# A head-major layout for score blocks that pass through DRAM, half as many small transfers, and a new written-out order in a recurrence kernel

## The chip, the core and the metric

One core of a Trainium2 chip runs the whole program. Its engines are TensorE (PE; PEld is its weight load), VectorE (DVE), ScalarE (ACT), GpSimd (POOL) and SyncE (SP). Each has its own instruction queue and works through it in order; they wait for each other through semaphores. DMAs are issued from the queues of SP, ACT and POOL and all run on the core's 16 DMA engines. The metric is the device time of one execution in microseconds (us), as the median of several runs.

## The reference

Three stages follow each other: a recurrence over 768 time steps, an attention with four experts, and a gated MLP with a mixing over time. The change touches the first.

```python
def _attn_ref(r, k, v, w, a, b):          # all [4, 8, 768, 40]
    state = zeros((B, H, D, D))
    for t in range(S):
        y[:, :, t] = einsum('bhd,bhde->bhe', rt, state)
        Sa = einsum('bhde,bhe->bhd', state, at)
        state_decay = state * wt[:, :, None, :] - einsum('bhd,bhe->bhde', Sa, bt)
        state = state_decay + einsum('bhd,bhe->bhde', vt, kt)
# x = y as [4, 768, 320]
# moe:  per expert e of 4: causal softmax attention (head width 64), ye = a @ v @ wo[e], top-2 gated sum
# moe2: h = relu(x @ w_in); u, v = halves; v_n = layer norm of v; (u * (w_spatial @ v_n + b)) @ w_out
```

## The kernel before, in words

The recurrence is computed in 12 steps g of 64 time positions. Each step has two half-steps s = 2g and 2g + 1 (two of the four batch entries each, side by side on the partitions), so there are 24 half-steps.

**Preparation of a half-step s.** POOL issues the loads `xw`, `xa`, `xk`. DVE computes the running products of the decays (`scan`, L171), `at` (L176), a reciprocal (L179), the scan backwards (`back`, L181) and `kb` (L186). PE computes the 64x64 score blocks of eight heads (`t`, L195: 64 matrix products that run two by two, so the order prints 32 of a pair as x32) and transposes `kb` (`x`, L235). ACT copies the blocks out of PSUM (`lb`, L207, into `la` and `lb`) and stores both to a DRAM tensor (`lo`, L212); SP fetches them from there (`l`, L223) into the tile `ls`, in which each partition holds one 32x32 matrix. DVE masks the other half of the blocks (`lk`, L200).

**Inversion.** Two steps form a unit k (SIZES), six in all. When the four half-steps of a unit have been fetched, POOL masks the matrices (`lm`, L227), and DVE inverts 128 triangular matrices at once in 30 rows, two instructions each (`sub`, L252 and L254). ACT transposes half of them (`xc`, L259) and stores them (`xo`, L267).

**The step g.** SP fetches the inverses into the tiles G and R (`gx`, L273). PE and ACT combine them (`ma` L281, `mae`, `mb` L294, `mbe` L299). The state goes from step to step through `lv` (L306), `w` (L312), `we` (ACT, L317), `u` (L324), `ue` (ACT, L330), `s` (L341) and `state` (DVE, L348 and L349). The outputs need `st` (L355), `vt` (L369), `vte` (ACT), `a` (L386, two pieces of 64 products), `am` (DVE, L391, two), `ys` (L402), `yk` (L411), `xs` (DVE, L418) and the store `out` (SP, L1072) to the DRAM tensor `xd`.

**What sets the order.** `Plan` (L34) is given every piece with an engine, a guessed cost and a due time, and writes out one order for each engine: among the pieces that could begin within SLACK of the earliest, the one that is due first. REACH is the guessed time until a transfer's data can be used, PEC a factor on the costs of PE's pieces, DUE the numbers from which the due times are made. The order is fixed when the program is built; on the chip, an engine whose next instruction has to wait waits.

Besides, each DMA that SP or ACT issues takes one of eight completion counters in turn (DMAHW0 to DMAHW7 in the rows of the order), and waits until the DMA that had this counter eight DMAs earlier has landed. These waits stand in the queue of the issuing engine.

After the recurrence, the weights of the attention (L589 to L642 on DVE, prepared while its last steps run) and then attention and MLP follow; they read `xd` one batch entry after the other (L735, L766).

Of the kernel before, what the change touches and what calls it, by code (L numbers as in the profile page):

```python
# [7 lines left out]
F32 = mybir.dt.float32  # L8
# [13 lines left out]
CT = 64  # L22
SIZES = (2,  2,  2,  2,  2,  2)
RINGS = {"f": 4, "xw": 3, "xa": 2, "xk": 2, "kb": 1, "rp": 1, "pp": 12, "at": 9, "lk": 9, "la": 3, "lb": 10, "kbt": 11, "ls": 2, "lt": 1, "xt": 1, "wsb": 1,
       "s0": 1, "rt": 1, "vut": 2, "am": 2, "xs": 1}
DUE = {"pace": 21.6, "lead": 66.3, "half": 2.6, "out": 1.0, "sub": 17.1, "row": 1.50, "turn": 17.7, "gx": 23.3, "load": 6.0, "init": 10.0}
LAG_US = 0.2
REACH = {"xw": 5.2, "xa": 5.2, "xk": 5.2, "v": 6.2, "r": 6.2, "lo": 5.5, "l": 5.5, "xo": 5.2, "gx": 5.7, "init": 1.2}
SLACK = 0.1
PEC = 0.71  # L30
QPR = 8


class Plan:  # L34
# [5 lines left out]
    def add(self, name, engine, cost, due, fn, needs=(), makes=None, uses=()):  # L40

        self.items[name] = [engine, cost * PEC if engine == "PE" else cost, due, fn, list(needs) + list(uses), makes, list(uses)]

    def order(self):
# [9 lines left out]
        def begin(n):  # L54
            engine, _, _, _, needs, makes, _ = items[n]
            if makes and len(rings[makes]) >= self.cap[makes]:
                needs = needs + readers.get(rings[makes][-self.cap[makes]], [])
                if any(u not in at for u in needs):
                    return None
            return max([free.get(engine, 0.0)] + [at[u] + REACH.get(u[0], 0.0 if items[u][0] == engine else LAG_US)  # L60
                                                  for u in needs])

        open_ = [n for n in items if not missing[n]]
        while open_:
            can = [(t, items[n][2], i, n) for i, n in enumerate(open_) for t in (begin(n),) if t is not None]
            first = min(can)[0]

            _, _, t, n = min((due, i, t, n) for t, due, i, n in can if t <= first + SLACK)
            free[items[n][0]] = at[n] = t + items[n][1]
# [11 lines left out]
def recurrence(ctx, tc, shape, x_in, rt_in, v_in, ident, store_x, pre=None):  # L81


    nc = tc.nc
    B, H, S, D = shape
    C, L2 = CT, CT // 2
# [9 lines left out]
    dp = ctx.enter_context(tc.tile_pool(name="rdram", bufs=1, space=DRAM))  # L96
# [3 lines left out]
    starts = [sum(SIZES[:k]) for k in range(len(SIZES))]  # L100
    unit_of = [k for k, n in enumerate(SIZES) for _ in range(n)]

    XW, XA, XK, LA, LO, PP, AT, KBT, KB, LK, LB, XT, RT, VU = ({} for _ in range(14))
    LS, LT, XO, pw, wsb, aq, rp = ({} for _ in range(7))
# [102 lines left out]
            nc.scalar.copy(d[s], aq["t", s][:, 1].rearrange("p (h t) -> p h t", h=H)[:, :, i * L2:(i + 1) * L2])  # L207

    def p_lo(s):
        LO[s] = dp.tile([2, 2, C, H, L2], F32, name=f"lo{s}")  # L210
        for i, t in enumerate((LA[s], LB[s])):
            nc.scalar.dma_start(LO[s][i].rearrange("y j h t -> (y j) h t"), t)  # L212

    def p_l(s):

        k = unit_of[s // 2]
        n = SIZES[k] * 32
        if k not in LS:
            LS[k] = ap.tile([128, L2, L2], F32, name="ls", bufs=RINGS["ls"])
        for y in range(2):  # L220
            for i in range(2):
                at0 = i * n + (s // 2 - starts[k]) * 32 + y * 16 + s % 2 * H
                nc.sync.dma_start(LS[k][at0:at0 + H], LO[s][i, y, i * L2:(i + 1) * L2].rearrange("j h t -> h j t"))  # L223

    def p_lm(k):
        n = 2 * SIZES[k] * 32
# [34 lines left out]
    def p_xo(g):  # L261
        k = unit_of[g]
        n = SIZES[k] * 32
        at0 = (g - starts[k]) * 32
        XO[g] = dp.tile([2, 2, 2 * H, L2, L2], F32, name=f"xo{g}")
        for i, t in ((1, LS[k][n:2 * n]), (0, LT[k][:n])):
            nc.scalar.dma_start(XO[g][i].rearrange("y n l t -> (y n) (l t)"), t[at0:at0 + 32].rearrange("n l t -> n (l t)"))  # L267

    def load_x(g):

        for y in range(2):
            for i, t in enumerate((G, R)):
                nc.sync.dma_start(t[rows(2 * y + i), :, i * L2:(i + 1) * L2],  # L273
                                  XO[g][i, y].rearrange("n l t -> l n t"))

    def m_a(g):
        aq["ma", g] = pt = bank2()
# [145 lines left out]
    add = plan.add  # L423
    last = NS - 1
    add(("init", 0), "POOL", 14.5, DUE["init"], lambda: init())
    for k, n in enumerate(SIZES):
        due = DUE["pace"] * starts[k] - DUE["lead"]
        ss = range(2 * starts[k], 2 * (starts[k] + n))
        for s in ss:
            d = due - DUE["half"] * (ss[-1] - s)  # L430
            add(("xw", s), "POOL", 1.2, d - DUE["load"], lambda s=s: load_w(s), makes="xw")
            add(("xa", s), "POOL", 1.2, d - DUE["load"] + 1, lambda s=s: load_a(s), makes="xa")
            add(("xk", s), "POOL", 2.4, d - DUE["load"] + 2, lambda s=s: load_k(s), makes="xk")
            add(("scan", s), "DVE", 1.27, d, lambda s=s: scan(s), makes="pp", uses=[("xw", s)])
            add(("at", s), "DVE", 0.65, d, lambda s=s: at(s), makes="at", uses=[("xa", s), ("scan", s)])
            add(("back", s), "DVE", 1.45, d, lambda s=s: back(s), [("scan", s)], makes="rp", uses=[("xw", s)])
            add(("kb", s), "DVE", 1.24, d, lambda s=s: kb(s), makes="kb", uses=[("xk", s), ("back", s)])
            free = [(n, (s - RINGS[r]) // 2) for n, r in (("ma", "lb"), ("lv", "lk"), ("w", "at")) if s >= RINGS[r]]
            add(("t", s), "PE", 1.75, d, lambda s=s: p_t(s), free, makes="f", uses=[("kb", s), ("at", s)])
            free = [("lo", s - RINGS["la"])] if s >= RINGS["la"] else []  # L440
            add(("lb", s), "ACT", 0.75, d, lambda s=s: p_lb(s), free, makes="lb", uses=[("t", s)])
            add(("lk", s), "DVE", 0.7, d, lambda s=s: p_lk(s), [("lb", s)], makes="lk", uses=[("t", s)])
            free = [("xo", starts[k - RINGS["ls"] + 1] - 1)] if k >= RINGS["ls"] else []
            add(("lo", s), "ACT", 0.8, d, lambda s=s: p_lo(s), uses=[("lb", s)])
            add(("l", s), "SP", 2.2, d, lambda s=s: p_l(s), free + [("lo", s)])
            free = [("yk", (s - RINGS["kbt"]) // 2, q2) for q2 in range(2) if s >= RINGS["kbt"]]
            add(("x", s), "PE", 1.45, d + 2, lambda s=s: p_x(s), free, makes="f", uses=[("kb", s)])
            add(("xe", s), "ACT", 0.8, d + 2, lambda s=s: p_xe(s), makes="kbt", uses=[("x", s)])
        add(("lm", k), "POOL", 1.8, due + DUE["sub"], lambda k=k: p_lm(k), [("l", s) for s in ss])
        for j in range(1, L2 - 1):  # L450
            add(("sub", k, j), "DVE", 0.32 + 0.0022 * (L2 - 1 - j) * j, due + DUE["sub"] + DUE["row"] * j, lambda k=k, j=j: sub(k, j),
                [("sub", k, j - 1) if j > 1 else ("lm", k)])
        free = [("xo", starts[k] - 1)] if k else []
        add(("xc", k), "ACT", 2.0, due + 30, lambda k=k: p_xc(k), [("sub", k, L2 - 2)] + free)
        for g in range(starts[k], starts[k] + n):
            add(("xo", g), "ACT", 0.8, due + 30, lambda g=g: p_xo(g), [("xc", k)])
    for g in range(NS):
        due, k, e, o = DUE["pace"] * g, unit_of[g], (2 * g, 2 * g + 1), DUE["pace"] * (g + 1) + DUE["out"]
# [10 lines left out]
            uses=[("lk", s) for s in e])  # L469
# [10 lines left out]
        for q2 in range(2):  # L480
# [5 lines left out]
                uses=[("am", g, q2), ("xe", 2 * g + q2)])  # L486
        add(("ys", g), "PE", 1.5, o + 2, lambda g=g: ys(g), [("a", g, 1), ("am", g, 0)], makes="f",
            uses=[("r", g), ("ste", g)])
        add(("xs", g), "DVE", 1.3, o + 3, lambda g=g: xs(g), [("yk", g, 0), ("yk", g, 1)], makes="xs",
            uses=[("ys", g)] + [("scan", s) for s in e])  # L490
        add(("out", g), "SP", 2.4, o + 3, lambda g=g: store_x(g * C, aq.pop(("xs", g))), uses=[("xs", g)])

    prep = None
    for name in plan.order():
# [232 lines left out]

def first_x(tc, xd, kx, st, xs):
    split = splitter(tc.nc)
    _, DM, S = xd.shape  # L730
    xs.append(x_tiles(kx, S))
    xh, xl = xs[0]
    for k, (k0, kn) in enumerate(chunks(DM)):
        xf = st.tile([128, S], F32, name="xf")
        tc.nc.sync.dma_start(xf[:kn], xd[0, k0:k0 + kn, :])  # L735
        for _ in range(XFW):
            yield 0.5
        split(xh[:kn, k], xl[:, k] if k < 2 else xh[64:, k], xf[:kn], None, True)
        yield 0.5


def moe_mlp(tc, xd, c, bank, E, HD, FF, out, ident, wk_, wk2, kx, x0, ml):

    nc = tc.nc
    split = splitter(nc)
    B, DM, S = xd.shape
    FH = FF // 2
    NT = S // 128
    KT = chunks(DM)
# [5 lines left out]
    xs, res, raw, prog, taken = {0: x0}, {}, {}, [(-1, 0)], [-1]  # L755
# [4 lines left out]
    def fetch_x(b):  # L760
        if b >= B:
            return
        raw[b] = []
        for k, (k0, kn) in enumerate(KT):
            xf = wk2.tile([128, S], F32, name=XFN, bufs=FB if XFN == "f" else 3)
            nc.sync.dma_start(xf[:kn], xd[b, k0:k0 + kn, :])  # L766
            raw[b].append(xf)

    def load_x(b):
# [290 lines left out]
def kernel_body(tc, shape, x_in, rt_in, v_in, w_gate, wq, wk, wv, wo, w_in, w_sp, b_sp, w_out, out):  # L1060
    nc = tc.nc
    B, H, S, D = shape
    with ExitStack() as top:
        cp = top.enter_context(tc.tile_pool(name="top", bufs=1))
        dp = top.enter_context(tc.tile_pool(name="xdram", bufs=1, space=DRAM))
        ident = cp.tile([128, 128], F32, name="ident")
        make_identity(nc, ident)
        xd = dp.tile([B, H * D, S], F32, name="xd")

        def store_x(t0, xs):  # L1070
            for q in range(B):
                nc.sync.dma_start(xd[q, :, t0:t0 + CT].rearrange("(h e) t -> e h t", h=H),  # L1072
                                  xs[q % 2 * 64:q % 2 * 64 + D, q // 2])

        E, _, HD = wq.shape
        FF = w_in.shape[1]
# [10 lines left out]
        with ExitStack() as ctx:  # L1087
# [5 lines left out]
            xs = []  # L1093
# [84 lines left out]
```

## Time and profile before

| | us |
|---|---|
| median of 3 runs (lowest to highest) | 966.35 (962.58 to 968.76) |
| the profiled execution | 961.51 |
| its span, first to last instruction | 959.8 |
| PE / DVE / ACT / POOL busy | 765.9 / 676.1 / 432.1 / 239.6 |
| DMA | 98,709 packets, 70.16 MB; 75,761 packets are under 512 B |

The busy times are sums over all stages. The recurrence ends at about 424 us; the rest of the span belongs to attention and MLP. What ends last in a stage is read from the waits of each engine in that stage and from its line of time.

### The profile page before, as it was taken

To read this page: it belongs to the slowest core of one execution; us is meant where nothing else is said; L and a number is where in the kernel's file an instruction comes from. 1 tells how busy PE (TensorE), PEld (TensorE's weight loads), DVE (VectorE), ACT (ScalarE), POOL (GpSimd) and SP (SyncE) were. 2 spreads that over 40 slices of the span, in tenths; PEclk is the share of its full clock that TensorE was granted. 3 is DMA by queue.
4 is the path that set the end of the run, shared out by engine and by line. 5 is a ranking of instruction groups with operands and counts; after the bars stand their busy time and mean duration, and the time that the engine had idled before them with its cause. 6 is when DMAs were issued, how large, how long until landed. Compare 5 with 4: busy or idle time off the path is not lost.

```text
span 959.8 us, 29495 instructions
## 1 busy us (share of the span) xinstructions
PE 765.9 (80%) x12496; PEld 688.2 (72%) x12496; DVE 676.1 (70%) x1581; ACT 432.1 (45%) x1053; POOL 239.6 (25%) x425
## 2 busy tenths in 40 slices
PE   4526688777867677757788879998799988999898
PEld 3515677667757576646566769997699976999798
DVE  8899867888786863339998786567865668556730
ACT  1113334333323333315787565565655646556522
POOL 5462222223110101017740022110321104111041
PEclk9999977977868968977799989998999988999999
DMA  7845565565462525243211000010000100000001
GB/s 212 215 134 130 138 146 136 148 156 159 116 142 63 129 58 116 70 122 102 75 50 42 2 1 1 22 56 8 1 1 22 56 8 1 1 22 15 8 1 42
DMA packets 98709, 70.16 MB, mean 73 GB/s; under 512 B 75761, under 2 KB 85233, under 8 KB 98578
## 3 DMA queue, kind: packets, MB, share of 16 engines
q0 software_dynamic: 11520, 33.13, 12.4%
q1 hardware_dynamic: 78994, 25.71, 11.9%
q10 hardware_dynamic: 8064, 9.44, 3.2%
q8 instruction: 98, 1.61, 0.7%
q14 instruction: 33, 0.27, 0.1%
HBM read 50.95 MB, written 17.30 MB: 71 GB/s over the span
## 4 chain that ended last, share of the span: by engine, by line
PE 51%; DVE 27%; DMA 8%; issue 7%; ACT 5%; SPq 1%; POOL 1%; ACTq 0%; DVEq 0%; POOLq 0%
PE mm L942 6%; PE mm L943 5%; PE mm L944 5%; DVE sub L252 4%; DVE ls L254 4%; PE mp L901 3%; PE mp L831 3%; PE f L386 2%; PE f L195 2%; PE f L369 2%; PE f L411 2%; PE f L341 2%; ACT f L871 2%; DMA ls<-lo 2%; DVE nm L866 2%
## 5 line engine op out<-in xcount | busy, mean ns | idle before, releaser
L195 PE MATMUL f<-at,kb 40*64 40x64 f32 x1536 | 41.9, 281 | 61.8 <-DVE kb L186 53.6
L195 PEld LDWEIGHTS f<-at,kb 40*64 40x64 f32 x1536 | 37.8, 189 | 66.0 <-issue 39.3
L871 ACT ACTIVATE f<-sc,nm 128x512 f32<-128x512 f32 (+3 forms) x128 | 68.8, 542 | 34.2 <-DVE nm L866 17.3
L592 DVE TENSOR_TENSOR ptl<-mp,pth 128x256 fp32r<-128x256 f32 (+2 forms) x144 | 65.5, 461 | 22.5 <-ACT pth L591 21.4
L866 DVE TENSOR_REDUCE nm<-sc 128x1 f32<-128x512 f32 (+3 forms) x128 | 63.0, 503 | 22.0 <-PE sc L864 18.5
L591 ACT CAST pth<-mp 128x256 fp32r<-128x256 f32 (+2 forms) x144 | 57.5, 408 | 32.4 <-PE mp L901 21.5
L901 PE MATMUL mp<-ident,f 128*128 128x128 f32 x336 | 60.1, 295 | 8.3 <-DVE f L887 4.2
L254 DVE TENSOR_TENSOR ls<-ls,sub 128x30 f32<-128x30 f32 (+9 forms) x180 | 61.4, 341 | 6.6
L252 DVE TENSOR_TENSOR sub<-ls 128x30 f32<-128x30 f32 (+9 forms) x180 | 61.0, 339 | 5.9 <-DMA ls<-lo 1.1
L910 PE MATMUL pa<-pth,vv 128*128 128x256 f32 x192 | 54.7, 299 | 10.1 <-DVE at L922 7.5
L912 PE MATMUL pa<-ptl,vv 128*64 128x256 f32 x192 | 51.4, 289 | 3.1 <-DVE ptl L592 2.8
L901 PEld LDWEIGHTS mp<-ident,f 128*128 128x128 f32 x336 | 42.1, 150 | 14.9 <-DVE f L887 7.2
L386 PE MATMUL f<-rt,vut 64*64 64x64 f32 x1536 | 35.7, 247 | 20.7 <-issue 20.6
L859 PE MATMUL sc<-kk,qq 128*128 128x512 f32 (+3 forms) x128 | 43.6, 378 | 10.6 <-ACT qq L835 5.4
L910 PEld LDWEIGHTS pa<-pth,vv 128*128 128x128 f32 x192 | 38.4, 200 | 17.1 <-DVE at L922 10.0
L942 PE MATMUL mm<-ws_h,vn_h 128*128 128x384 f32 x144 | 49.4, 343 | 0.4 <-ACT vn_h L591 0.3
L943 PE MATMUL mm<-ws_l,vn_h 128*128 128x384 f32 x144 | 48.7, 338 | 0.0
L386 PEld LDWEIGHTS f<-rt,vut 64*64 64x64 f32 x1536 | 32.0, 159 | 22.9 <-issue 22.6
L944 PE MATMUL mm<-ws_h,vn_l 128*128 128x384 f32 x144 | 48.4, 336 | 0.0
L887 DVE TENSOR_SCALAR f<-f,sm 128x128 f32<-128x128 f32 (+2 forms) x96 | 45.2, 512 | 3.8 <-POOL sm L879 3.1
L391 DVE TENSOR_TENSOR am<-f,mask 128x1024 f32<-128x1024 f32 x24 | 28.9, 1221 | 26.8 <-PE f L386 26.7
L207 ACT COPY la<-f 128x256 f32<-128x256 f32 x24 | 9.0, 374 | 82.2 <-PE f L195 82.2
(230 smaller groups left out, 2359.4 us busy)
## 6 DMA issues: line engine op xcount, KB each, us to landing
xk<-in_x_dram POOLq DMA_DIRECT2D x48, 208.0 KB, 4.5
rt<-in_rt_dram POOLq DMA_DIRECT2D x24, 256.0 KB, 3.9
VU<-in_v_dram POOLq DMA_DIRECT2D x24, 256.0 KB, 4.5
xw<-in_x_dram POOLq DMA_DIRECT2D x24, 211.7 KB, 4.5
xa<-in_x_dram POOLq DMA_DIRECT2D x24, 208.0 KB, 4.4
xd<-xs SPq DMA_DIRECT2D x48, 80.0 KB
out_dram<-ob SPq DMA_DIRECT2D x24, 160.0 KB
lo<-la ACTq DMA_DIRECT2D x24, 128.0 KB
```

The source lines that it names most:

```text
L195: nc.tensor.matmul(pt[half(z ^ j), j, h * C:(h + 1) * C], KB[s][half(z, D), h, z ^ j], AT[s][half(z, D), h], start=(h == 0), stop=True, sk ...
L252: nc.vector.tensor_mul(tv, X[:, :m, j:j + 1].to_broadcast([m_, m, n]), X[:, j:j + 1, j + 1:].to_broadcast([m_, m, n]))
L254: nc.vector.tensor_sub(X[:, :m, j + 1:], X[:, :m, j + 1:], tv)
L386: nc.tensor.matmul(pa[half(j), h, i * C:(i + 1) * C], t[half(h), i, j * C:(j + 1) * C], RT[g][half(h), p, 2 * q2 + z], start=(i == 0), sto ...
L592: (lo_eng or nc.vector).tensor_sub(lo, src, hi.bitcast(F32))
L866: nc.vector.tensor_reduce(nm[:, z:z + 1], sc[:, :nn], op=OP.max, axis=AX.X, negate=True)
L871: nc.scalar.activation(pe[:, n0:n0 + nn], scs[z][:, :nn], AF.Exp, bias=nm[:, :1], accum_out=sm[:, z, i - i0:i - i0 + 1])
L901: nc.tensor.transpose(pp[:, j, z * 128:(z + 1) * 128], pes[z][:, (j0 + j) * 128:(j0 + j + 1) * 128], ident)
L910: nc.tensor.matmul(pa[:, c0:], vv[:, j0 + j, e].rearrange("p a h -> p (a h)"), pth[:, j, c0:], start=(j0 + j == 0), stop=False, skip_group ...
L942: nc.tensor.matmul(ps_, ah, bh, start=first, stop=False)
L943: nc.tensor.matmul(ps_, ah, bl_, start=False, stop=False)
L944: nc.tensor.matmul(ps_, al, bh, start=False, stop=last)
```

## The change

Four things change.

The DRAM tensor `lo` of a half-step is laid out by head: [2, H, 2C, 32] in place of [2, 2, C, H, 32]. The two stores of a half-step then write 1,024 runs of 128 B each, where they wrote 128 runs of 1 KB, and the fetch has two DMAs of 16 rows of 4 KB, where it had four DMAs of 256 runs of 128 B. The rows of `ls` come in another order within their 32, and `XO` and `load_x` follow that.

`xd` has its batch axis split in two, and the output of a step is stored in two DMAs in place of four, with the same runs of 256 B.

The planner's numbers change, and so the order of all five engines. The costs given for `l` and `out` on SP are smaller.

The readers of `xd` use its new shape.

```diff
-DUE = {"pace": 21.6, "lead": 66.3, "half": 2.6, "out": 1.0, "sub": 17.1, "row": 1.50, "turn": 17.7, "gx": 23.3, "load": 6.0, "init": 10.0}
+DUE = {"pace": 21.7, "lead": 62.1, "half": 6.2, "out": 3.9, "sub": 18.0, "row": 1.39, "turn": 6.2, "gx": 22.2, "load": 8.0, "init": -1.8}
-REACH = {"xw": 5.2, "xa": 5.2, "xk": 5.2, "v": 6.2, "r": 6.2, "lo": 5.5, "l": 5.5, "xo": 5.2, "gx": 5.7, "init": 1.2}
-SLACK = 0.1
-PEC = 0.71
+REACH = {"xw": 4.5, "xa": 4.5, "xk": 4.5, "v": 5.5, "r": 5.5, "lo": 4.8, "l": 4.8, "xo": 4.5, "gx": 5.0, "init": 0.5}
+SLACK = 0.05
+PEC = 0.98
...
     def p_lo(s):
-        LO[s] = dp.tile([2, 2, C, H, L2], F32, name=f"lo{s}")
+        LO[s] = dp.tile([2, H, 2 * C, L2], F32, name=f"lo{s}")
         for i, t in enumerate((LA[s], LB[s])):
-            nc.scalar.dma_start(LO[s][i].rearrange("y j h t -> (y j) h t"), t)
+            nc.scalar.dma_start(LO[s][i].rearrange("h p t -> p h t"), t)
...
-        for y in range(2):
-            for i in range(2):
-                at0 = i * n + (s // 2 - starts[k]) * 32 + y * 16 + s % 2 * H
-                nc.sync.dma_start(LS[k][at0:at0 + H], LO[s][i, y, i * L2:(i + 1) * L2].rearrange("j h t -> h j t"))
+        for i in range(2):
+            at0 = i * n + (s // 2 - starts[k]) * 32 + s % 2 * 16
+            nc.sync.dma_start(LS[k][at0:at0 + 16].rearrange("n l t -> n (l t)"),
+                              LO[s][i].rearrange("h (y j) t -> (h y) (j t)", y=2)[:, i * L2 * L2:(i + 1) * L2 * L2])
...
-        XO[g] = dp.tile([2, 2, 2 * H, L2, L2], F32, name=f"xo{g}")
+        XO[g] = dp.tile([2, 4 * H, L2, L2], F32, name=f"xo{g}")
...
-                                  XO[g][i, y].rearrange("n l t -> l n t"))
+                                  XO[g][i].rearrange("(n y) l t -> y l n t", y=2)[y])
...
-            add(("l", s), "SP", 2.2, d, lambda s=s: p_l(s), free + [("lo", s)])
+            add(("l", s), "SP", 0.9, d, lambda s=s: p_l(s), free + [("lo", s)])
...
-        add(("out", g), "SP", 2.4, o + 3, lambda g=g: store_x(g * C, aq.pop(("xs", g))), uses=[("xs", g)])
+        add(("out", g), "SP", 1.0, o + 3, lambda g=g: store_x(g * C, aq.pop(("xs", g))), uses=[("xs", g)])
...
-        xd = dp.tile([B, H * D, S], F32, name="xd")
+        xd = dp.tile([2, B // 2, H * D, S], F32, name="xd")
...
-            for q in range(B):
-                nc.sync.dma_start(xd[q, :, t0:t0 + CT].rearrange("(h e) t -> e h t", h=H),
-                                  xs[q % 2 * 64:q % 2 * 64 + D, q // 2])
+            for z in range(2):
+                nc.sync.dma_start(xd[z, :, :, t0:t0 + CT].rearrange("q (h e) t -> e (q h) t", h=H),
+                                  xs[z * 64:z * 64 + D].rearrange("e q h t -> e (q h) t"))
```

**ACT, at the start.** The queue of ACT from the copies of the third half-step to the stores of the fourth, before and then in the change. What stands in brackets is what the row waits for; DMAHW are the completion counters.

```order
L207 COPY la<-f 128x256 [waits PE_49]
L207 COPY lb<-f 128x256
L212 DMA lo_324<-la 128x256 [waits DMAHW4_49,Activation_49]
L212 DMA lo_324<-lb 128x256 [waits DMAHW5_49,Activation_49]
L242 COPY kbt<-f 128x320 [waits PE_49]
L242 COPY kbt<-f 128x320
L207 COPY la<-f 128x256 [waits DMAHW0_49,PE_49]
L207 COPY lb<-f 128x256
L212 DMA lo_398<-la 128x256 [waits DMAHW2_49,Activation_49]
L212 DMA lo_398<-lb 128x256 [waits DMAHW3_49,Activation_49]
```

```order
L207 COPY la<-f 128x256 [waits PE_49]
L207 COPY lb<-f 128x256
L212 DMA lo_320<-la 128x8x32 [waits DMAHW0_49,Activation_49]
L212 DMA lo_320<-lb 128x8x32 [waits DMAHW1_49,Activation_49]
L242 COPY kbt<-f 128x320 [waits PE_49]
L242 COPY kbt<-f 128x320
L207 COPY la<-f 128x256 [waits PE_49]
L207 COPY lb<-f 128x256
L212 DMA lo_394<-la 128x8x32 [waits DMAHW4_49,Activation_49]
L212 DMA lo_394<-lb 128x8x32 [waits DMAHW5_49,Activation_49]
```

A half-step issues six DMAs before (two stores, four fetches) and four in the change. Before, the counters of the fourth half-step's stores were last used by fetches of the second; in the change those of a store were last used by a store two half-steps earlier.

**DVE, late in the inversion of the fourth unit, around the two `am` and the `lk` of one step.** Before, and then in the change.

```order
L254 TENSOR_TENSOR ls<-ls,sub 128x19x12
L391 TENSOR_TENSOR am<-f,mask 128x1024
L200 TENSOR_TENSOR lk<-f,mask 128x512
L391 TENSOR_TENSOR am<-f,mask 128x1024
L252 TENSOR_TENSOR sub<-ls 128x220
...
L254 TENSOR_TENSOR ls<-ls,sub 128x22x9
L348 TENSOR_TENSOR ST_88<-ST_89,f 104x8x40
L349 TENSOR_TENSOR ST_88<-ST_88,pp 104x8x40
```

```order
L391 TENSOR_TENSOR am<-f,mask 128x1024
L252 TENSOR_TENSOR sub<-ls 128x198
...
L254 TENSOR_TENSOR ls<-ls,sub 128x25x6
L200 TENSOR_TENSOR lk<-f,mask 128x512
L391 TENSOR_TENSOR am<-f,mask 128x1024
L252 TENSOR_TENSOR sub<-ls 128x130
L254 TENSOR_TENSOR ls<-ls,sub 128x26x5
L348 TENSOR_TENSOR ST_88<-ST_89,f 104x8x40
L349 TENSOR_TENSOR ST_88<-ST_88,pp 104x8x40
```

The rows of the inversion now stand between the first `am` and the `lk`, where the two `am` and the `lk` followed each other. At its first inversion DVE also begins three instructions earlier in its order: `at`, the reciprocal and `back` of the eighth half-step come behind the inversion's first 18 rows now.

**PE, step 10, from the product with the state (`w`) to the next state's product (`s`).** Before, and then in the change. The 32 rows of `ys` (L402) are left out.

```order
L312 MATMUL f<-ST_88,at 64x40 x32
L281 MATMUL f<-G,lb 32x32 x32
L386 MATMUL f<-rt,vut 64x64 x64
L294 MATMUL f<-R,G 64x64 x32
...
L411 MATMUL f<-am,kbt 40x64 x16
L324 MATMUL f<-wsb,xt 64x40 x32
L411 MATMUL f<-am,kbt 40x64 x16
L355 MATMUL f<-ident,ST_88 128x104 x8
L337 LDWEIGHTS scan_79
L337 MATMUL f<-scan_79 128x320
...
L341 MATMUL f<-VU_90,kbt 40x40 x32
```

```order
L312 MATMUL f<-ST_88,at 64x40 x32
L294 MATMUL f<-R,G 64x64 x32
L386 MATMUL f<-rt,vut 64x64 x32
L324 MATMUL f<-wsb,xt 64x40 x32
L386 MATMUL f<-rt,vut 64x64 x32
L337 LDWEIGHTS scan_79
L337 MATMUL f<-scan_79 128x320
...
L341 MATMUL f<-VU_90,kbt 40x40 x32
L355 MATMUL f<-ident,ST_88 128x104 x8
...
L411 MATMUL f<-am,kbt 40x64 x32
```

`ys` and `yk` of the step before stand ahead of `s` in the old order and behind it in the new one; `ma` has moved ahead of `w`.

## Rows read from the trace of the kernel before

**Rows 1.** Stretches: us; busy time and count by engine; granted clock, DMA share, GB/s.

```profile
0.00:72.00 72.00, 29.89 (x584) 26.55 (x584) 61.32 (x112) 13.21 (x36) 39.38 (x70) 1.00 0.68 187
72.00:323.00 251.00, 187.99 (x6469) 172.57 (x6472) 198.76 (x397) 86.17 (x164) 55.14 (x95) 0.84 0.55 133
323.00:424.00 101.00, 71.60 (x2615) 65.94 (x2607) 49.34 (x108) 31.25 (x49) 8.67 (x19) 0.83 0.37 81
424.00:960.00 536.00, 476.38 (x2842) 423.11 (x2842) 366.72 (x966) 301.43 (x806) 136.41 (x242) 0.94 0.09 28
```

**Rows 2.** Waits of DVE, 72 to 323 us: total us, times, longest.

```profile
DVE ST L348 <- PE f L341: 15.4, 6, 4.0
DVE lk L200 <- ACT lb L207: 10.7, 6, 2.8
DVE am L391 <- PE f L386: 9.2, 7, 2.7
...
DVE kb L186 <- PE f L235: 0.2, 1, 0.2
```

**Rows 3.** Waits of DVE, 0 to 72 us.

```profile
DVE lk L200 <- ACT lb L207: 2.8, 1, 2.8
DVE sub L252 <- DMA ls<-lo: 1.1, 1, 1.1
```

**Rows 4.** Line of time at the start: begin, length, engine, instruction, wait before it.

```profile
29.70 0.33 ACTq L212 DMA_DIRECT2D lo<-la  x1
39.18 0.33 ACTq L212 DMA_DIRECT2D lo<-lb  x1
45.46 1.45 POOL L227 TENSOR_SCALAR_AFFINE_SELECT ls<-ls 128x1024 f32<-128x1024 f32 x1 [6.21 <-DMA ls<-lo]
46.95 0.19 DVE L252 TENSOR_TENSOR sub<-ls 128x30 f32<-128x30 f32 x1 [1.11 <-DMA ls<-lo]
```

**Rows 5.** The chain of waits at the start: begin, length, what.

```profile
12.38 3.70 DMA lo<-la
...
73.83 2.00 DMA xo<-lt
76.32 3.83 DMA R<-xo
```

**Rows 6.** Issues by line: shortest, median, longest ns in the issuing queue.

```profile
L212 ACTq DMA_DIRECT2D lo<-lb x24: 326/391/1779, 12.8 to 305.3; - x24
L273 SPq DMA_DIRECT2D G<-xo x24: 303/404/1594, 75.9 to 383.9; - x24
```

**Rows 7.** The page's DMA queues: packets, MB, share of 16 engines' span.

```profile
q1 hardware_dynamic: 78994, 25.71, 11.9%
q8 instruction: 98, 1.61, 0.7%
```

**Rows 8.** Waits of PE, 100 to 323 us.

```profile
PE f L386 <- issue: 11.4, 8, 3.0
PE f L195 <- DVE kb L186: 7.1, 4, 4.2
...
PE f L294 <- ACT G L287: 1.3, 1, 1.3
...
PE f L341 <- issue: 0.4, 1, 0.4
```

**Rows 9.** Line of time of the last steps.

```profile
360.15 1.09 PE L411 MATMUL f<-am,kbt 128*40 128x64 f32 x32
379.29 0.30 DVE L589 CAST wv_h<-wvg 128x260 fp32r<-128x260 f32 x1 [4.88 <-DMA wvg<-in_moe_w_gate_dram]
383.70 2.36 DVE L391 TENSOR_TENSOR am<-f,mask 128x1024 f32<-128x1024 f32 x2
391.48 0.49 DVE L348 TENSOR_TENSOR ST<-ST,f 104x320 f32<-104x320 f32 x1 [1.98 <-PE f L341]
418.65 1.29 DVE L418 TENSOR_TENSOR xs<-f,pp 104x512 f32<-104x512 f32 x2 [2.61 <-PE f L411]
```

More of the change, by code (lines that the diff above doesn't have):

```diff
@@ L264, in p_xo @@
         at0 = (g - starts[k]) * 32
-        XO[g] = dp.tile([2, 2, 2 * H, L2, L2], F32, name=f"xo{g}")
+        XO[g] = dp.tile([2, 4 * H, L2, L2], F32, name=f"xo{g}")
         for i, t in ((1, LS[k][n:2 * n]), (0, LT[k][:n])):
-            nc.scalar.dma_start(XO[g][i].rearrange("y n l t -> (y n) (l t)"), t[at0:at0 + 32].rearrange("n l t -> n (l t)"))
+            nc.scalar.dma_start(XO[g][i].rearrange("n l t -> n (l t)"), t[at0:at0 + 32].rearrange("n l t -> n (l t)"))
     def load_x(g):
@@ L729, in first_x @@
     split = splitter(tc.nc)
-    _, DM, S = xd.shape
+    _, _, DM, S = xd.shape
     xs.append(x_tiles(kx, S))
@@ L734, in first_x @@
         xf = st.tile([128, S], F32, name="xf")
-        tc.nc.sync.dma_start(xf[:kn], xd[0, k0:k0 + kn, :])
+        tc.nc.sync.dma_start(xf[:kn], xd[0, 0, k0:k0 + kn, :])
         for _ in range(XFW):
@@ L745, in moe_mlp @@
     split = splitter(nc)
-    B, DM, S = xd.shape
+    B, DM, S = 2 * xd.shape[1], *xd.shape[2:]
     FH = FF // 2
@@ L765, in fetch_x @@
             xf = wk2.tile([128, S], F32, name=XFN, bufs=FB if XFN == "f" else 3)
-            nc.sync.dma_start(xf[:kn], xd[b, k0:k0 + kn, :])
+            nc.sync.dma_start(xf[:kn], xd[b % 2, b // 2, k0:k0 + kn, :])
             raw[b].append(xf)
```

## The prediction, made before the changed kernel ran

> **What bounds the kernel now.** The profiled execution took 961.51 us, 1.7 us more than its span, and lies 4.8 us below the median of 966.35; the sum below is made against 961.51 and shifted by 4.8 at its end. I read the busy times by stretch first [rows 1]. Three stretches cover the recurrence. Up to 72 us DVE is busy for 61.3 of 72 us. From 72 to 323 us, which holds the inversions of the second to the fifth unit and all that DVE does between them, DVE is busy for 198.8 of 251 us and PE for 188.0, at a granted clock of 0.84. From 323 to 424 us PE is busy for 71.6 of 101 us and DVE for 49.3. What follows is untouched but for the shape of `xd`, and I count nothing there.
>
> Then I read the waits. DVE spends 42.7 us of the long stretch in seven kinds of waits [rows 2]; the three largest, for the next state, for copied score blocks and for the products of `am`, are 35.3. The reader is to see that all but one of the shown rows wait for PE: DVE has the most work, but PE hands it over late. PE itself waits for 29.9 us in nine rows whose releaser is "issue", and for 21.0 us in seven rows that name another engine or a DMA [rows 8], of which the first and the last of each kind are shown. So neither engine is full. DVE loses time where PE's piece stands too far behind in PE's order or too early in DVE's, and that is what an order can change.
>
> **The start.** The first inversion begins at 46.95, after a wait of 1.1 us for fetched blocks, and `lk` waited 2.8 us before it [rows 3, 4]. The line of time shows why. ACT stored `la` of the fourth half-step at 29.70, and a later store of `lb` went out only at 39.18, with the copies for which `lk` waited behind it; the order shows that ahead of such a store ACT waits for a completion counter that a fetch last used. In the change four DMAs a half-step take counters, not six, and a store's counter was last used by a store two half-steps earlier. I take both waits away: −3.9 us. DVE would then come to its first `sub` at 46.95 − 3.9 = 43.0, and three instructions earlier still, at about 41, since `at`, the reciprocal and `back` of the eighth half-step come later; these only change places and are worth nothing. Can the data be there by 41? A store issued a little over 1 us earlier than that 29.70, at some 28.4, lands 3.7 us later, a fetch of 4 KB rows takes about 2.0 us as `xo` does [rows 5], or 3.8 as the 512 runs of R do; POOL's mask takes 1.45 [rows 4]. That is 35.6 to 37.4, so the sum holds even with a few us of lateness. POOL's own work that moves behind the mask is covered by the first inversion, which lasts to about 70 us.
>
> **The store with 1,024 runs.** No row shows a store in runs of 128 B. From below, it lands as now, 3.7 us. From above, I go by the fetches: the queue with most small packets spends 0.119 × 16 × 959.8 / 78,994 = 23.1 ns on a packet [rows 7]. The change turns 6,144 runs of 1 KB and 24,576 of 128 B into 49,152 of 128 B and 768 of 4 KB. The 24,576 more of 128 B come to 24,576 × 23.1 / 16 = 35 us of all 16 engines over 24 half-steps, 1.5 us a half-step, and the 6,144 runs of 1 KB that fall away give some of that back. In the long stretch the DMA engines are busy to 0.55, so there is room, and a block has a whole half-step of some 251 / 16 = 15.7 us to get through. I take 0, with 1.5 us at the start as the other end. The start's spare above takes that as well.
>
> [...]
>
> **Issues.** A store's issue holds ACT's queue for 0.39 us in the median, and a fetch of 512 runs holds SP's for 0.40 [rows 6]: the number of runs hardly counts there, so I keep 0.39 for 1,024 runs. The longest that a store held it is 1.78, which is the other end. On SP, 48 issues of `l` and 24 of `out` fall away. SP is not waited for in these rows except through data, so that is worth 0, and is cover for nothing.
>
> **The order, 72 to 323 us.** DVE's work stays the same instructions, 198.8 us, about 50 per unit, and its waits are 10.7 per unit. The new order puts rows of the inversion between the first `am` and `lk`, so that PE has some 1 us per pair of rows more for the products. On PE `s` now stands ahead of `ys` and `yk` of the step before, which answers to the largest wait, 15.4 us for the next state. [...] The ends per unit are 0 and 10.7. I take 5, half of the old: the state wait should nearly go, those of `lk` and `am` should halve, and some will come back at `xs`, whose products now stand later. Over four units that is 20 us left of 42.7: −22.7.
>
> **The tail.** Between the steps 9 and 10, DVE's preparation of attention weights waits 7.8 us in two waits for gate weights (the larger is shown), and `am` begins only at 383.70; PE's order has `u` of the next step behind `yk`, which waits for that `am`, and the state comes at 391.48 [rows 9]. With `u` and `s` ahead of `yk`, the state waits only for DVE's own queue: `am` of 2.36 us and `xs` of 1.29 bring it to 387.3, −4.2. If the gate weights land earlier as well, 7.8 more: −12. I take −6, nearer to the first, since nothing in the change moves those loads far. At the end, two pieces of `yk` of 1.09 each and some 1.2 us of `ys` stand behind the last `s` and ahead of the last `xs` (now at 418.65): +3.4. Together −2.6.
>
> **Sum.** −3.9 − 22.7 − 2.6 = −29.2: 932.3 us, or 937 beside the median.
>
> **Rivals.** [...]
>
> *The order does not do what it says.* DVE's waits move from `state` to `xs` and `am` and stay at 42.7, since what is released in one place is taken in the next. Then only the start and the tail are left, −6.5, or less where a late block eats the start: 960 to 966. For it: the planner's guessed costs, not measured ones, set both orders. Against it: no new wait can be named in the order that would be worth 20 us.
>
> *Slower: the stores hold ACT.* If an issue of 1,024 runs takes the longest time seen, 1.78 us, in place of 0.39, ACT's queue stands for 1.39 us more at each of the 32 stores that 16 half-steps issue after 72 us: 44.4 us. `we`, `ue` and `mbe` stand behind them in ACT's queue, PE waits for those, and DVE for PE. With all of it on the path, −29.2 + 44.4 = +15, or 982. It decides from an issue of 0.39 + 29.2 / 32 = 1.30 us, where the gain is gone. Against it: the median for 512 runs, and that ACT is busy for only 86 of 251 us, so a part would be hidden.
>
> **How the numbers follow.** This kernel's runs scatter by some 6 us, so within 1% (9.7 us) counts as no change. The forecast, DVE's waits falling to between 2.5 and 8 us per unit, has a chance of 0.62 and covers 925 to 949 by 2.5 × 4 = 10 us better and 3 × 4 = 12 us worse. PE as the bound has 0.12 (949), the order without effect 0.14 (960 to 966), and the slower case 0.12 (982). The range reaches from 912, where all of DVE's waits in the long stretch go (−20 more) and the tail comes near its end at −12 (−5 more), to 964, which takes in most of the case without effect and leaves the slower one out. Faster by over 1% are the first two cases less 0.01 that may end nearer: 0.73; within 1% is the case without effect, with that 0.01 and less 0.01 in which it turns out worse: 0.14; slower by over 1% is the rest: 0.13.
>
> **What would show it.** Right: the first `sub` between 41 and 44 us, no wait for a counter ahead of the fourth half-step's stores; DVE's waits near 5 us per unit, with those for the state nearly gone; the state of step 10 some 20 us after that of step 9; store issues of about 0.4 us. Wrong: store issues above 1.3 us, new waits of `lm` or of the first `sub` for blocks that landed late, or DVE's waits unchanged and only renamed. [...]

## The result, and the profile after

The changed kernel takes 940.3 us in the median (938.16 to 943.25), against 967.56 of the kernel before in runs beside it: a ratio of 0.972, with an interval of 0.966 to 0.978. The forecast was 937, in a range of 912 to 964. The profiled execution took 940.45 us, with a span of 938.7.

I cut the span at three events that both orders have: the end of the first inversion (the begin of its last row), that of the fifth, and the begin of the last `xs`. They are rows of the line of time (71.31, 322.23 and 418.65 us before; 68.60, 296.34 and 394.71 after).

| stretch | before | after | difference | forecast |
|---|---|---|---|---|
| to the end of the first inversion | 71.3 | 68.6 | −2.7 | −3.9 |
| from there to the end of the fifth | 250.9 | 227.7 | −23.2 | −22.7 |
| to the last `xs` | 96.4 | 98.4 | +2.0 | −2.6 |
| attention and MLP | 541.2 | 544.0 | +2.8 | 0 |
| span | 959.8 | 938.7 | −21.1 | −29.2 |

The last stretch runs the same instructions; over all profiled runs of this study it took 541 to 547 us. The profiled execution of before is at the low end of its runs, which is why the medians differ by more (27 us) than the two profiles.

**The long stretch** of the changed kernel, in the columns of [rows 1]:

```profile
68.80:296.54 227.74, 172.83 (x6190) 156.00 (x6191) 196.29 (x395) 82.40 (x156) 52.28 (x89) 0.89 0.61 140
```

DVE is busy for 196.3 us there, 2.5 less than before, with 395 instructions for 397; PE's granted clock is 0.89 where it was 0.84. DVE's waits there, all rows but one of 0.5 us:

```profile
DVE am L391 <- PE f L386: 7.8, 6, 2.9
DVE xs L418 <- PE f L411: 6.2, 4, 2.6
DVE ST L348 <- PE f L341: 6.0, 5, 2.0
DVE lk L200 <- ACT lb L207: 1.9, 2, 1.2
```

They answer to [rows 2]: 22.4 us are left of 42.7, where I had taken 20. The waits for the state and for `lk` fell by 9.4 and 8.8 us; those of `am` hardly moved. So 20.3 of the 23.2 us are waits that went, and 2.5 that DVE is busy for less. PE's two largest waits in the same stretch:

```profile
PE f L195 <- DVE kb L186: 11.6, 4, 9.7
PE f L386 <- issue: 10.9, 6, 5.1
```

[rows 8] begin at 100 us; from 72 to 323 us the first of the two was, before:

```profile
PE f L195 <- DVE kb L186: 16.2, 5, 9.1
```

PE's waits for "issue" came to 33.9 us in this stretch and to 31.3 in the one of before: they did not shrink, and the time did.

**The start.** The fourth half-step's stores go out right behind the copies now, where [rows 4] had 29.70. ACT's line of time, then the chain of waits, then POOL and DVE:

```profile
27.43 0.37 ACTq L212 DMA_DIRECT2D lo<-la  x1
27.90 1.17 ACTq L212 DMA_DIRECT2D lo<-lb  x1
```

```profile
27.90 5.58 DMA lo<-lb
33.49 5.75 DMA ls<-lo
```

```profile
39.75 2.26 POOL L227 TENSOR_SCALAR_AFFINE_SELECT ls<-ls 128x1024 f32<-128x1024 f32 x1 [2.98 <-DMA ls<-lo]
42.05 0.19 DVE L252 TENSOR_TENSOR sub<-ls 128x30 f32<-128x30 f32 x1 [1.11 <-POOL ls L227]
```

The counter waits are gone and the first `sub` is 4.9 us earlier; some 2 us of that are the three instructions that come later now. DVE's wait of 2.8 us for `lk` [rows 3] is gone too. Its wait of 1.1 us just ahead of the first `sub` stayed: what it waits for is POOL's mask, which in [rows 4] also ends right ahead of that `sub`. The store took 5.58 us and the fetch 5.75, where I had put 3.7 and 2.0 to 3.8 [rows 5].

**Issues and queues**, against [rows 6] and [rows 7]:

```profile
L212 ACTq DMA_DIRECT2D lo<-lb x24: 366/568/1423, 12.8 to 289.9; - x24
```

```profile
q1 hardware_dynamic: 54946, 25.71, 10.9%
q10 hardware_dynamic: 51072, 9.44, 5.5%
```

Of a half-step's two stores of 1,024 runs, the second (shown) holds ACT for 0.57 us in the median and 1.42 at most, the first for 0.37: the slower case, which needed 1.3, did not come. The 49,152 short runs are on q10, at 0.055 × 16 × 938.7 / 51,072 = 16.2 ns a packet, where I had priced them at 23.1. What the change halves is the number of fetch and output DMAs; the packets under 512 B rose from 75,761 to 100,097.

**The tail.** The line of time of DVE, against [rows 9]:

```profile
302.00 0.19 DVE L252 TENSOR_TENSOR sub<-ls 128x30 f32<-128x30 f32 x1 [3.84 <-POOL ls L227]
342.04 0.49 DVE L348 TENSOR_TENSOR ST<-ST,f 104x320 f32<-104x320 f32 x1 [7.08 <-PE f L341]
362.25 0.49 DVE L348 TENSOR_TENSOR ST<-ST,f 104x320 f32<-104x320 f32 x1 [1.34 <-PE f L341]
375.99 1.23 DVE L391 TENSOR_TENSOR am<-f,mask 128x1024 f32<-128x1024 f32 x1 [8.59 <-PE f L386]
394.71 1.29 DVE L418 TENSOR_TENSOR xs<-f,pp 104x512 f32<-104x512 f32 x2 [2.58 <-PE f L411]
```

The last state, of step 10, comes 29 us earlier than the one at 391.48, and 20.2 us behind that of step 9, as forecast; but 32.5 us pass from it to the last `xs`, 27.2 before: more of the outputs are left for the end.

### The profile page after: what moved, and what is told of

It is laid out like the page before. It is cut to its first block, busy times and chain, and to the rows that moved or that the text cites. A ratio compares the mean times of both kernels' runs of the same rounds, so it can differ in the third digit from the quotient of the medians.

```text
span 938.7 us, 29407 instructions
## 1 busy us (share of the span) xinstructions
PE 762.6 (81%) x12496; PEld 681.2 (73%) x12496; DVE 672.4 (72%) x1581; ACT 431.7 (46%) x1053; POOL 243.1 (26%) x425
## 3 DMA queue, kind: packets, MB, share of 16 engines
q10 hardware_dynamic: 51072, 9.44, 5.5%
## 4 chain that ended last, share of the span: by engine, by line
PE 51%; DVE 27%; issue 7%; ACT 7%; DMA 4%; ACTq 1%; POOL 1%; SPq 1%; DVEq 0%; POOLq 0%
PE mm L942 6%; PE mm L943 6%; PE mm L944 5%; DVE sub L252 4%; PE mp L901 3%; DVE ls L254 3%; PE mp L831 3%; PE f L386 3%; PE pa L910 2%; PE f L411 2%; PE sc L859 2%; PE pa L912 2%; ACT f L871 2%; PE f L195 2%; DVE nm L866 2%
## 5 line engine op out<-in xcount | busy, mean ns | idle before, releaser
L871 ACT ACTIVATE f<-sc,nm 128x512 f32<-128x512 f32 (+3 forms) x128 | 68.9, 542 | 35.3 <-DVE nm L866 19.8
L391 DVE TENSOR_TENSOR am<-f,mask 128x1024 f32<-128x1024 f32 x24 | 29.2, 1222 | 29.5 <-PE f L386 29.4
L592 POOL TENSOR_TENSOR vn_l<-vr,vn_h 128x512 fp32r<-128x512 f32 x21 | 26.7, 1299 | 74.6 <-ACT vn_h L591 57.6
```

Of the source, the lines that this page charges most:

```text
L592: (lo_eng or nc.vector).tensor_sub(lo, src, hi.bitcast(F32))
L871: nc.scalar.activation(pe[:, n0:n0 + nn], scs[z][:, :nn], AF.Exp, bias=nm[:, :1], accum_out=sm[:, z, i - i0:i - i0 + 1])
```

## The experiments

Runs beside each other share the runs of before; its medians were 966.1 (first four), 966.0 (next four), 967.0 (next three) and 966.0 us (the last). The table has, from each run's line of time, the ends of the first and the fifth inversion and the last `xs`, and the stretch between the first two.

| kernel | median | ratio to before (interval) | end 1 | end 5 | stretch | last `xs` |
|---|---|---|---|---|---|---|
| before (the profiled run) | | | 71.3 | 322.2 | 250.9 | 418.7 |
| changed | 940.3 | 0.972 (0.966 to 0.978) | 68.6 | 296.3 | 227.7 | 394.7 |
| e1, new DMAs, old order | 959.6 | 0.993 (0.989 to 0.996) | 68.6 | 318.0 | 249.4 | 414.5 |
| e2, new order, old DMAs | 939.5 | 0.973 (0.967 to 0.980) | 71.9 | 296.9 | 225.1 | 392.6 |
| e3, changed, four fetches | 939.8 | 0.973 (0.967 to 0.980) | 68.7 | 298.2 | 229.4 | 396.1 |
| e4, changed, mask ahead | 942.8 | 0.977 (0.970 to 0.984) | 68.7 | 293.9 | 225.2 | 396.2 |
| e5, changed, r once | 939.9 | 0.974 (0.970 to 0.978) | 68.5 | 298.7 | 230.2 | 393.0 |
| e6, before, PE move | 975.7 | 1.010 (1.006 to 1.015) | 75.3 | 331.4 | 256.1 | 430.9 |
| e7, before, DVE spread | 965.7 | 1.000 (0.996 to 1.003) | 75.1 | 327.6 | 252.5 | 422.0 |
| e8, before, both moves | 971.4 | 1.007 (1.004 to 1.011) | 72.2 | 328.9 | 256.7 | 427.1 |
| e9, before, factor 0.98 | 947.5 | 0.981 (0.975 to 0.988) | 74.3 | 303.3 | 229.0 | 402.1 |
| e10, changed, factor 0.90 | 945.1 | 0.978 (0.972 to 0.985) | 68.9 | 300.3 | 231.3 | 398.8 |
| e11, changed, factor 1.10 | 955.2 | 0.990 (0.984 to 0.995) | 68.8 | 295.7 | 227.0 | 407.2 |
| e12, changed, bunched | 949.1 | 0.983 (0.978 to 0.988) | 71.1 | 309.4 | 238.3 | 403.1 |

**e1: the DMA parts alone.** The changed kernel with the old `DUE`, `REACH`, `SLACK`, `PEC` and the old costs of `l` and `out`:

```diff
-DUE = {"pace": 21.7, "lead": 62.1, "half": 6.2, ...}
+DUE = {"pace": 21.6, "lead": 66.3, "half": 2.6, ...}
-PEC = 0.98
+PEC = 0.71
```

> The new layouts and DMAs (4 KB fetches, two output stores, four DMAs a half-step) with the old planner numbers, so every compute engine has its old order. Theory A (the order gives the gain): only the start gets better, first sub at 42 to 44 us against 46.95; DVE's waits in the long stretch stay at 35 to 43 us, lk's near 10; total 3 to 6 us under before, about 962. Theory B (fewer DMAs and freed counters give the gain, the lk waits being ACT held by counters): lk's waits fall from 10.7 to under 3, total 15 us or more under before, about 948.

It gained 7 us, a little more than theory A's 3 to 6, and far from theory B. The first inversion ends as early as in the changed kernel, the long stretch is as long as before, and the waits for `lk` are not less but more (one of 6.9 us, which I have not explained):

```profile
DVE lk L200 <- ACT lb L207: 15.5, 6, 6.9
DVE ST L348 <- PE f L341: 12.4, 5, 3.7
```

So the `lk` waits of [rows 2] were not ACT being held by counters. That held ACT at the start only: in the kernel before its waits put down to DMAs are 18.6 us up to 72 us and 2.7 from there to 323.

**e2: the order alone.** The kernel before with the new numbers and the new costs of `l` and `out`; layouts and DMAs are old:

```diff
-PEC = 0.71
+PEC = 0.98
-            add(("l", s), "SP", 2.2, ...)
+            add(("l", s), "SP", 0.9, ...)
```

> The new planner numbers with the old layouts and all old DMAs, so every compute engine has the changed kernel's order. Theory A: DVE's waits in the long stretch fall to 20 to 26 us as in the changed kernel, the first sub stays at 46 to 48 us; total 17 to 22 us under before, about 946. Theory B: the counters hold ACT in the new order too, DVE waits 35 us or more, total under 8 us below before, about 960.

It is as fast as the changed kernel, not some 6 us behind it as theory A had it, and DVE's waits in the long stretch are 19.9 us. The first inversion waited for its blocks, and ended 3.3 us later than in the changed kernel:

```profile
45.32 0.19 DVE L252 TENSOR_TENSOR sub<-ls 128x30 f32<-128x30 f32 x1 [4.47 <-POOL ls L227]
```

By the end of the fifth inversion 0.6 us of that was left, and the last `xs` came 2 us sooner. In the new order the early start buys nothing; in the old one (e1) it bought all that the layouts have to give. The gain of the change is the order's, whole.

**e3: the counters with the new layout.** Each half-step's fetch in four DMAs:

```diff
-            nc.sync.dma_start(LS[k][at0:at0 + 16]...
+            for z in (0, 8):
+                nc.sync.dma_start(LS[k][at0 + z:at0 + z + 8]...
```

> The changed kernel, but each half-step's fetch split into four DMAs of 8 rows of 4 KB, so that six DMAs a half-step take completion counters again, with the new runs. If the start's gain comes from the counters: waits ahead of the fourth half-step's stores are back, first sub at 45 to 48 us, total 3 to 6 us above the changed kernel, about 944. If it comes from the fetch's long runs: first sub at 42, total as the changed kernel, 940.

First `sub` at 42.18 and the same total, as the run-length side expected. The counter waits did come back: the second store of the fourth half-step goes out at 28.43, just behind the landing of a fetch, where it went at 27.90, and ACT waits 7.5 us in three waits for fetches at the next half-steps. But they are short, since the two fetches on the chain of waits at the start land in 4.73 and 5.96 us, where the old ones took 6.52 and 9.76. e2 has the same order, six DMAs and old fetches, and its first `sub` is 3.1 us later; on the two chains, 2.7 of that are the last fetch itself (8.66 us against 5.96) and 1.1 the store that a counter held longer; the rest gives 0.6 back. The number of counters taken is not what held the start; how long the fetches take is.

**e4: the last unit's mask ahead of two loads on POOL.** In the changed kernel DVE waits 3.84 us for it at 302.00, and POOL shows why: it was behind a load of r that waited 18 us for PE.

```profile
297.64 1.11 POOL L131 DMA_DIRECT2D rt<-in_rt_dram  x2 [18.02 <-PE f L411]
300.69 1.28 POOL L227 TENSOR_SCALAR_AFFINE_SELECT ls<-ls 128x1024 f32<-128x1024 f32 x1
```

```diff
+    for name in (("v", 9), ("r", 7)):
+        names.remove(name)
+        names.insert(names.index(("lm", 5)) + 1, name)
```

> The changed kernel, but the mask of the last unit (lm 5) stands ahead of the loads r 7 and v 9 on POOL, behind which it waited until 300.7 us. If those two loads held it: DVE's 3.8 us wait before the last inversion falls under 1 us, the last state comes 2 to 4 us earlier, total about 937. Rival: PE bounds the end, the last output comes at the same time, 940. Second rival: the blocks of the last half-step landed late, the wait stays.

The wait went and the last inversion began 5.6 us earlier, at 296.41; it ended at 331.75, where it had ended at 331.12. DVE waited for `am` in its midst instead (waits of DVE, 293 to 332 us):

```profile
DVE am L391 <- PE f L386: 8.7, 2, 8.2
```

In the changed kernel DVE's waits for `am` are 2.3 us there. The wait that was removed came back whole, at the next products that DVE needed from PE.

**e5: r loaded once.** It tests whether the waits for `am` in the tail are held by the load of r; the other eleven loads are left out.

```diff
+        if g:
+            RT[g] = RT[0]
+            return
```

> The changed kernel, but r is loaded only for the first step and used in all twelve: the other eleven loads of r are left out (the output is then another one). Theory C: with ys behind s the tile of r comes free late, its next load waits, and the first product a waits for that load; so in the changed kernel's tail DVE's waits for a (8.6 and 3.8 us around step 10) are the load of r. Expected: these two fall under 2 us together, last output 6 to 10 us earlier, total 930 to 934. Rival (PE bounds the tail, its issue waits stay): the waits move to xs, total 938 to 941.

Theory C falls. The two waits around step 10, 8.6 and 3.8 us in the changed kernel, stay at 6.68 and 3.42, and so does the time:

```profile
376.00 1.23 DVE L394 TENSOR_TENSOR am<-f,mask 128x1024 f32<-128x1024 f32 x1 [6.68 <-PE f L389]
380.64 1.23 DVE L394 TENSOR_TENSOR am<-f,mask 128x1024 f32<-128x1024 f32 x1 [3.42 <-PE f L389]
```

**e6, e7, e8: the moves that the prediction named, made in the old order.** e6 puts `ys` and `yk` of a step behind the next `s` and `xs` behind the state, at the `s` of steps 3, 5, 7 and 9 (by the line of time the changed kernel has this at the steps 1, 2, 3, 5, 7 and 10, and not at 4, 6, 8 and 9); e7 puts four `lk` and five second `am` behind rows of the inversion; e8 does both.

```diff
+    for g in range(3, 11, 2):   # e6
+        for after, late in ((("s", g), [("ys", g - 1), ("yk", g - 1, 0), ("yk", g - 1, 1), ("r", g)]),
+                            (("state", g), [("xs", g - 1), ("out", g - 1)])):
...
+    for n, k in [(("lk", s), 5) for s in range(8, 24)] + [(("am", g, 1), 3) for g in range(1, 9)]:   # e7
...
```

> The kernel before with one move only: in the steps 3, 5, 7 and 9 PE's ys and yk of the step before go behind s, and xs behind the state on DVE. Theory A: the state waits of the steps 5, 7 and 9 (2.7, 4.0, 1.2 us) fall under 1 us each; total 4 to 8 us under before, about 960. Rival (waits are only renamed): xs or am takes them over, total within 2 us of before.

> The kernel before with DVE's moves only: where rows of the inversion follow directly, four lk and five second am go behind up to five and three of those rows. Theory A: the waits of these lk (1.3 and 2.4 to 2.8 us for some) fall, total 2 to 5 us under before, about 963. Rival: what DVE does not wait there it waits at the next state, total within 1.5 us of before.

> The kernel before with the moves of the two kernels beside it together. Theory A, gains that add up: 6 to 12 us under before, about 957. Rival (one makes room for what the other loses): no better than the better of the two. Either way it stays well short of the changed kernel's 940, since the half-steps' own places and the end of the inversions are not moved.

None gained. e6 is slower by 1.0%, which neither side expected, e8 by 0.7%, and e7 is the same. Of the 12.3 us by which e6's last `xs` is late, 4.0 stand ahead of the end of the first inversion, where none of its moves lies (the last section comes back to this); 5.1 are the long stretch. DVE's waits of e6 from 71.5 to 335 us:

```profile
DVE lk L200 <- ACT lb L207: 12.7, 6, 6.4
DVE am L391 <- PE f L386: 11.2, 8, 2.5
DVE ST L348 <- PE f L341: 11.0, 6, 2.9
DVE xs L418 <- PE f L411: 10.0, 4, 5.2
```

The states of the steps 5 and 7 did come sooner after those ahead of them (23.1 and 20.8 us after them, 24.4 each before), and the waits for the state fell from 15.4 to 11.0. The next step gave it back: from the state of step 5 to that of step 6 42.0 us passed, 39.6 before. `xs`, `lk` and `am` wait more. My theory of the single moves fell with this, as far as these places go: at the steps 1 and 2 the move was not tried.

**e9: the planner's factor alone.**

```diff
-PEC = 0.71
+PEC = 0.98
```

> The kernel before with one number changed: the planner's factor on PE's costs, 0.71 to 0.98; old due times, layouts and DMAs. Theory D, formed after the single moves gave nothing: the gain is in how evenly DVE's work is dealt out between one state and the next. Before, the steps 5, 7 have 18 and 16 us of DVE's work and the steps 6, 8 have 37 and 34, so PE's chain from state to state doesn't fit into the short ones and PE idles in the long ones; with the factor alone it is 25, 30, 25, 24. Theory D expects DVE's waits between the first and the fifth inversion near 22 us (42.7 before), total 938 to 948. Rival (the due times make the gain): 957 to 966.

One number brings 19 of the 27 us. The long stretch is 229.0 us, 22 shorter than before, with 24.2 us of waits, the first three of which are:

```profile
DVE ST L348 <- PE f L341: 10.0, 4, 5.4
DVE am L391 <- PE f L386: 7.0, 3, 3.1
DVE lk L200 <- ACT lb L207: 4.0, 2, 3.6
```

The rest of its distance to the changed kernel is mostly ahead of the stretch: its first inversion ends at 74.3, not at 68.6. In its order `ys` stands ahead of the next `s` at every step, as before; of `yk`, a half has gone behind the `s` of steps 1, 2, 3, 9 and 10 as well, where before it had at 5 and 7. So the move that I had put first is not needed for the gain, but for those halves of `yk`.

What the factor does is to price PE's pieces. From the page of the changed kernel:

```profile
L195 PE MATMUL f<-at,kb 40*64 40x64 f32 x1536 | 41.4, 279 | 53.4 <-DVE kb L186 44.4
L386 PE MATMUL f<-rt,vut 64*64 64x64 f32 x1536 | 37.0, 249 | 17.0 <-issue 14.4
```

Both are 24 pieces of 64: 1.73 us for a `t`, 1.54 for an `a`. The planner prices them at 1.75 and 1.8 times the factor: 1.24 and 1.28 us at 0.71, 1.72 and 1.76 at 0.98. Not all pieces fit so well: an `s` took 1.84 us (20.2 us for eleven) and is priced at 1.07 and 1.47.

**e10 and e11: the factor at 0.90 and at 1.10**, in the changed kernel.

```diff
-PEC = 0.98
+PEC = 0.9
```

> The changed kernel with the factor at 0.90: the steps 5 to 8 then have 18, 38, 19, 25 us of DVE's work between the states, where it is 22, 32, 22, 26 at 0.98. Theory D: waits rise to 28 us or more, total 946 to 956. Rival (due times make the gain): 938 to 942.

> The changed kernel with the factor at 1.10: 30, 24, 30, 17 us of DVE's work in the steps 5 to 8, a step less uneven than at 0.98 but for the last. Theory D: waits at or under 22 us, total 933 to 941. Rival: 0.98 is a lucky order and any other is worse, 946 or more.

Theory D fails in its own terms. e10 deals out DVE's work about as unevenly as before (18, 38, 19, 25 us), and its long stretch is 231.3 us with 22.9 of waits; its total of 945.1 lies between theory D's 946 and the rival's 942. e11 deals it out less unevenly and has a stretch of 227.0 us with 24.3 of waits, no better than the changed kernel's; its loss comes after the fifth inversion, where DVE waits for the last unit's mask again and twice as long (DVE's waits from there to 405 us):

```profile
DVE am L391 <- PE f L386: 22.7, 7, 7.9
DVE sub L252 <- POOL ls L227: 8.0, 1, 8.0
```

So from 0.90 to 1.10 the long stretch is the same within 4.3 us, and the totals differ by what each order leaves for the end. In the totals e11's rival was right: 0.98 is the best of the three orders, and 955 is over its 946. And the stretch is as short at 1.10, where `t` and `a` are priced at 1.93 and 1.98 us: what these runs show is that prices well under the measured times cost, not that a close fit is needed. A factor of 0.71 with the new due times was not run.

**e12: the half-steps bunched again.** In DUE, `half` is the distance between the due times of a unit's half-steps and `lead` how far ahead of its steps they are due.

```diff
-DUE = {"pace": 21.7, "lead": 62.1, "half": 6.2, ...}
+DUE = {"pace": 21.7, "lead": 66.3, "half": 2.6, ...}
```

> The changed kernel with two old due numbers, half 2.6 and lead 66.3, and all else new, the factor 0.98 among it. This bunches the preparation of half-steps as before: between the kb of the units 4 and 5 lie 31 and 29 us of DVE's work and then 7 to 9 us each, where the order before has 32, 6, 7, 8 and all orders with a factor from 0.90 up have at most 25 us. But am stays 9 to 15 us of DVE's work behind the state, as in those orders, where it was 4 to 10 before. Theory F (the spread of half-steps is what the factor brings): the stretch from the first to the fifth inversion's end is back at 240 us or more, DVE's waits over 30 us, total 950 or more. Theory G (the distance from PE's products to DVE's use of them is): stretch 226 to 232 us, waits 20 to 26, total 937 to 946.

It came out between the two: waits of 33.5 us as theory F expected, a stretch of 238.3 and a total of 949.1 just short of it, and both over theory G's.

```profile
71.28:309.56 238.28, 178.94 (x6192) 162.51 (x6192) 195.68 (x395) 81.83 (x156) 49.21 (x87) 0.86 0.57 134
```

So an order with bunched half-steps loses 10.5 of the 23 us again. That the factor gains these by spreading them is argued from this and not shown, since the two numbers move other pieces too, and with the factor at 0.98 the same two numbers gave 229.0 us in e9. Which moves are worth the rest stays open.

## Why the prediction was right, and where its steps failed

**The size was right and the reason for it was not.** That DVE's waits were what an order could take away held: the term for the long stretch was −22.7 us and measured −23.2, of which 20.3 are waits; 20 us of waits left were forecast and 22.4 measured. That the two agree so closely is luck, since half of the old waits was a middle between two ends. But I gave the gain to two places in the order, `s` ahead of `ys` and `yk`, and rows of the inversion around `am` and `lk`. e6 and e7 made moves of these two kinds, at some of the places, and gained nothing, and e9 gained 21.9 us in this stretch with `ys` ahead of `s` throughout. The step that failed is "On PE `s` now stands ahead of `ys` and `yk` of the step before, which answers to the largest wait". What the runs show in its place is that the planner's price of PE's pieces alone gives 21.9 of the 23.2 us; e12 suggests that about half of it is the spread of the half-steps. The split by rows was off as well: I had the state's wait nearly gone (it is 6.0), `am` halved (7.8 of 9.2) and `lk` halved (1.9 of 10.7).

**The start** was right in its mechanism and wrong as a term of the sum. The counter waits ahead of the fourth half-step's stores went and the first `sub` came at 42.05, inside 41 to 44. Of the two waits that I took away, for −3.9, only the one of 2.8 us for `lk` went; the one of 1.1 for POOL's mask stayed, and −2.7 was measured. The fetch was mis-sized, 5.75 us against 2.0 to 3.8 (the 2.0 was that of a store, `xo` from `lt`), and so was the store, 5.58 against 3.7 to 5.2. And e2, without any of it, is as fast. A term ahead of a stretch with another bound does not add to it.

For the stores in runs of 128 B I had taken 0, with 1.5 us at the start as the other end. They did cost time in the stores' queue. In the kernel before the queue's row was:

```profile
q10 hardware_dynamic: 8064, 9.44, 3.2%
```

That is 0.032 × 16 × 959.8 = 491 us over the 16 engines, 826 in the changed kernel (5.5%), so 335 / 16 / 24 = 0.9 us more a half-step in this queue. The landing times do not settle it: on the chains of waits at the start, six stores with runs of 128 B took 5.26 to 6.77 us (in the changed kernel, e1, e3, e4 and e10), those with runs of 1 KB 3.70 to 5.40 in the kernel before and e2, but 6.39 and 10.05 in e9 and 7.31 and 8.57 in e8.

**The tail** failed by 4.6 us: +2.0 where −2.6 was forecast. Up to the last state it gave 3.3 us, not 6: the state did not come to wait "only for DVE's own queue", since that of step 9 waited 7.08 us for PE and that of step 10 another 1.34, and the last inversion waited 3.84 us for its mask. Behind the last state it cost 5.3, not 3.4. e4 and e5 show that this stretch did not yield to the removal of one wait.

**The rivals.** The slower one is out: issues of 0.37 and 0.57 us in the median. The order without effect is out by the waits, 22.4 us of 42.7, and by e2. PE as the bound, at 949, is out: its waits for "issue" came to 33.9 us where they had been 31.3, and the stretch lost 23 all the same. No run shows the term behind that 949: over the orders these waits came to between 21.8 us (e11) and 39.7 (e9), in stretches of 227.0 and 229.0. What stands behind them is not shown; q8, the queue of instructions, fetched 98 packets before [rows 7] and after. The clock does not account for the gain either: the granted clock of the long stretch was 0.84 in e9 and 0.80 in e11, with stretches of 229.0 and 227.0 us, and 0.84 before with 250.9. Nor does the clock follow how much PE idles in [rows 1]: it is 1.00 with PE busy for 29.9 of 72 us, 0.84 for 188.0 of 251, 0.83 for 71.6 of 101 and 0.94 for 476.4 of 536.

One slip of the working has no weight: from 937, 10 us better is 927 and not 925.

## What to carry to other kernels

A wait that ends last in a row of the profile tells where time is lost, not which neighbour to move: moving one instruction group past another in a written-out order passed the wait on to the next step here. Where a planner writes the order, check first whether its prices lie under the measured time of the pieces; here one factor brought some 70% of the gain. Two gains found in separate parts of a program need not add: the early start was worth 7 us in the old order and nothing in the new one.

## What was not expected of the hardware

With old layouts and the old order at the start, the first `sub` began at 46.95, 47.83, 49.67, 50.51 and 50.72 us in five profiles with the same DVE instructions up to there (before, e8, e9, e7, e6). With the new layout and the new order it was 41.74 to 42.18 in six (e12, whose order puts more ahead of it, has 48.46). Completion counters that wait for a fetch make the start depend on when that fetch lands: in the kernel before, stores of ACT went out at 23.46 and 39.18 us, just behind fetches that landed at 23.38 and 39.10 and had taken 6.52 and 9.76; in e6 and e7 the fetches took 12.83 and 12.99. So the old starts of single profiles differ by up to 3.8 us, and the totals are compared by medians.
